# S4 convolution beside a SiLU feed-forward: the order of late loads on SyncE, a third weight landing buffer, and another split of the response's buffers

## The chip, the cores and the metric

The kernel runs on one core of one Trainium2 chip. The time is device microseconds (us) of one execution, taken as the median of three runs. Before the change it is 1117.28 us, and the three runs lie between 1115.24 and 1118.36 us. The profile was taken on one more execution, which took 1118.75 us.

The core has a matrix engine (TensorE, PE in the profile; PEld is its weight load), an elementwise engine (VectorE, DVE), an engine for activations and copies (ScalarE, ACT), GpSimd (POOL, used here to issue DMAs) and SyncE (SP, which only issues DMAs). Each engine takes its instructions in the order in which they were put into its queue. An instruction that waits holds up everything behind it on the same engine.

## The reference, cut to what matters

```python
xn = layernorm(x)                       # x: 2048 rows of 576
# A: S4 convolution over the 2048 positions, one filter per channel
K  = einsum("dn,dnl,dn->dl", C, exp(dt*A*l), dt*B).real      # 576 filters of length 2048
ya = irfft(rfft(pad(xn)) * rfft(pad(K)))[:2048] + xn * Dskip
# B: feed-forward, 576 -> 4608 -> 576
yb = silu(xn @ w1) @ w2
return x + ya + yb
```

## The kernel before, in words

**Feed-forward, the main thread.** The 2048 rows are worked in two halves of 1024, each half in two blocks of 512. The hidden width 4608 is cut into 9 chunks of 512, each of four pieces (`t` = 0 to 3) of 128. The loop goes over 36 blocks (half, chunk, block). `up` (lines 331 to 352) multiplies by `w1` into PSUM (`ph`) and applies SiLU (`gf`). `down` (lines 354 to 376) multiplies by `w2` into PSUM (`po`) and adds into the rows' accumulator (`acc`). All products are made of high and low parts, so a weight tile is split once it has landed: ScalarE casts the high part (`w1h`, line 303; `w2h`, line 324), VectorE subtracts for the low part (`w1l`, line 305; `w2l`, line 326). While one block is in `down`, `up` of the next block is already being made.

**Weights.** `load_w1` (line 274) brings two pieces of `w1` at a time into `w1r` with three DMAs on SyncE; it has one landing buffer. `load_w2` (line 310) brings one piece of `w2`, 288 KB, into `w2r` with one DMA on SyncE; it has two landing buffers, so a load waits until the split of the piece two places ahead has read its buffer. For the last chunk of the second half, the pieces 2 and 3 of `w2` and the second part of `w1` land in another pool (`yp`) instead. That pool takes the memory of the convolution's middle stage (`kl`), so those loads cannot start before that stage is over. All six weight loads of the last chunk are put into the program together, while the chunk before it is still at work (lines 435 to 438).

**Convolution, the side thread.** It is woven into the feed-forward at fixed fractions of its steps (`weave`, line 33, and `marks` and `tail_at` in `side`). Its stages are: layernorm and transposes; the filters (`kgen`), written to DRAM as `d1k`; the spectral stage (`spectral`, line 742); and the tail (`tail`, line 894). The spectral stage makes 16 visits `p`. In each, `load_k` fetches rows of `d1k` on GpSimd's queue, `halves` combines them on VectorE into `k` with one operation on line 782 and two on line 784, `response` multiplies `k` on TensorE (`pk`, line 795), `inputs` does the same for the data, and `back` writes a result to DRAM (`d2`, line 851). In the tail, `conv_load` (line 926) fetches rows of `d2` into a tile `ys` by two DMAs on SyncE, `load_r0` (line 898) fetches finished rows of the first half, and `add_conv` (line 935) makes the last small products (`py`, line 944) and adds them (line 952).

**What sets the order.** A scheduler orders the instructions of each engine when the program is built. An instruction can be tied to come after another one on the same engine: `behind(ins)`. The first eight `conv_load` calls and two `load_r0` calls of the tail stand in such a block:

```python
        with behind(pins["load"]):
            for j in (0, None, 2, None, None, None, None, None):
                conv_load()
                if j is not None:
                    load_r0(j)
```

`pins["load"]` is the weight load that was written last into the program at that time. Before the change every `load_w1` and `load_w2` sets it, and the last to do so ahead of the tail is piece 3 of the last chunk's `w2`. The tie only says that these loads come after that one load; it says nothing about the pieces of `w2` that were written earlier into the program and still wait for a landing buffer.

Of the kernel before, what the change touches and what calls it, by code (L numbers as in the profile page):

```python
# [11 lines left out]
F32 = mybir.dt.float32  # L12
# [3 lines left out]
ALU = mybir.AluOpType  # L16
# [3 lines left out]
P = 128  # L20
L = 2048
D = 576
# [21 lines left out]
def kernel(  # L44
# [22 lines left out]
    nc = tc.nc  # L67
    FT = 4
# [13 lines left out]
    d1k = dram.tile([32 * P, D], F32, name="d1k")  # L82
# [23 lines left out]
    wp = ctx.enter_context(tc.tile_pool(name="wp", bufs=2))  # L106
# [43 lines left out]
    pins = {}  # L150

    def behind(ins):
        return tc.issue_after(ins) if ins is not None else nullcontext()
# [113 lines left out]
    def ffn():  # L267
        w2v = w2.rearrange("(t p) d -> p t d", p=P)
# [5 lines left out]
        def load_w1(half, c, t):  # L274

            f = c * FT + t
            first = half == 0 and c == 0
            last = half == 1 and c == NCH - 1
            r1 = (pa if first and t else yp if last and t else wp).tile([P, 5, 2 * P], F32, tag="w1r", name="w1r", bufs=1)
            fs = slice(f * P, (f + 2) * P)  # L280
            v1 = w1[0:512, fs].rearrange("(k p) f -> p k f", p=P)
            eng = nc.sync
            if first and t == 0:
                eng = nc.scalar
                nc.sync.dma_start(r1[:, 0:2, :], v1[:, 0:2])
                eng.dma_start(r1[:, 2:4, :], v1[:, 2:4])
            else:
                nc.sync.dma_start(r1[:, 0:4, :], v1)  # L288
            if first and t == 0:
                eng = nc.gpsimd  # L290
            (eng if first and t == 0 else nc.sync).dma_start(r1[0:64, 4, :], w1[512:576, fs])  # L291
            pins["load"] = eng.dma_start(r1[64:128, 4, :], w1[512:576, fs]).ins  # L292
            R1[half, c, t] = r1

        def split_w1(half, c, t):
# [14 lines left out]
        def load_w2(half, c, t):  # L310

            first = half == 0 and c == 0
            last = half == 1 and c == NCH - 1
            r2 = (pa if first and t > 1 else yp if last and t > 1 else wp).tile([P, D], F32, tag="w2r", name="w2r", bufs=2)
            pins["load"] = nc.sync.dma_start(r2, w2v[:, c * FT + t, :]).ins  # L315
            R2[half, c, t] = r2

        def split_w2(half, c, t):
# [68 lines left out]
        def split_xt(b, kt):  # L387
            xh, xl, x4 = xts[2 + b]
            with behind(pins["gh"]):
# [3 lines left out]
                else:  # L393
                    r4 = R4.pop(b)
                    nc.scalar.copy(x4, r4)
                    nc.vector.tensor_sub(x4[64:, :], r4[64:, :], x4[64:, :])

        load_w1(0, 0, 0)
        yield 0
        load_w1(0, 0, 2)  # L400
        yield 0
        split_w1(0, 0, 0)
        yield 0
        split_w1(0, 0, 2)
        for t in range(FT):
            load_w2(0, 0, t)
# [12 lines left out]
        for i, blk in enumerate(blocks):  # L419
            half, c, b = blk  # L420
# [3 lines left out]
            if half == 0 and c == NCH - 1:  # L424
                next_xt(b)

            after = {
                (0, "u0"): [(load_w1, 0)],
                (0, "u1"): [(split_w1, 0), (load_w2, 0), (load_w2, 1)],
                (0, "u2"): [(load_w1, 2)],  # L430
                (1, "u0"): [(split_w1, 2), (split_w2, 0), (load_w2, 2)],
                (1, "d3"): [(split_w2, 1), (load_w2, 3), (split_w2, 2)],
                (1, "u2"): [(split_w2, 3)],
# [10 lines left out]
            for step in ("u0", "d0", "d1", "d2", "d3", "u1", "u2", "u3"):  # L444
                k = int(step[1])
# [12 lines left out]
    kl = yp = pa = tail_at = None  # L458
# [283 lines left out]
    def spectral():  # L742

        uv = d1u.rearrange("(m p r) d -> p r m d", m=2, r=P)
        kv = d1k.rearrange("(m p r) d -> p m r d", m=2, r=P)
        cwt = kl.tile([P, 16, 3], F32, name="cwt", bufs=1)
        nc.sync.dma_start(cwt, cw)
        us, ks, mats, kab, ys = {}, {}, {}, {}, {}
# [6 lines left out]
        def load_k(p):  # L755
            if p > 15:
                return
            t = kl.tile([P, 2, D], F32, tag="k", name="k")
            w = kl.tile([P, 2, D], F32, tag="kw", name="kw", bufs=1)
            nc.gpsimd.dma_start(t[:, 1], kv[p, 0])  # L760
            nc.gpsimd.dma_start(w[:, 0], kv[p, 1])
            for r in range(4):
                nc.gpsimd.dma_start(w[32 * r:32 * r + 32, 1], kv[p, 1, 32 * (r ^ 1):32 * (r ^ 1) + 32])
            ks[p] = t, w

        def load_m(p, i):
            if p > 15:
# [9 lines left out]
        def halves(p):  # L777
            if p > 15:
                return
            t, w = ks[p]  # L780
            c = cwt[:, p]
            nc.vector.scalar_tensor_tensor(w[:, 0], w[:, 1], c[:, 0:1], w[:, 0], op0=ALU.mult, op1=ALU.add)
            for m in range(2):
                nc.vector.scalar_tensor_tensor(t[:, m], w[:, 0], c[:, 1 + m:2 + m], t[:, 1], op0=ALU.mult, op1=ALU.add)

        def visit(p, t, name):

            banks = psb.tile([P, 2, 2, 512], F32, tag="psb", name=name)
            last = pins["pe"]
            for n, (h, g) in enumerate(((0, 1), (0, 0), (1, 1), (1, 0))):  # L790
                gs = slice(64 * g, 64 * g + 64)
                for o in range(4):
                    os = slice(32 * o, 32 * o + 32)
                    with tc.high_priority(), behind(last):
                        last = nc.tensor.matmul(banks[os, g, h, :HD], mats[p, 0][gs, os], t[gs, o % 2, h * HD:(h + 1) * HD],
                                                start=True, stop=True, tile_position=(64 * g, 32 * o),
                                                skip_group_check=True).ins
            pins["pe"] = last
            return banks

        def response(p):

            kas = [kl.tile([P, D], F32, tag="ka", name="ka") for _ in range(2)]
            clear(visit(p, ks.pop(p)[0], "pk"), kas)
            for g in range(2):
                ka, kb = kas[g], kl.tile([P, D], F32, tag="kb", name="kb")
                nc.scalar.mul(kb[:64], ka[64:], -1.0)
                nc.scalar.copy(kb[64:], ka[64:])
                nc.scalar.copy(ka[64:], ka[:64])
                kab[2 * p + g] = ka, kb  # L810

        def clear(banks, dsts):

            with tc.high_priority():
                for g in range(2):
                    nc.scalar.copy(dsts[g].rearrange("p (h d) -> p h d", h=2), banks[:, g, :, :HD])
# [36 lines left out]
        def load_u2(p):  # L853
            if p < 16:
                load_u(p)

        load_k(0)
        load_m(0, 0)
        load_u(0)
        yield 1.0  # L860
        with behind(pins["gh"]):
            halves(0)
        load_m(0, 1)
        load_m(1, 0)
        yield 1.03
        load_k(1)
        load_u(1)
        yield 1.05
        response(0)
        yield 1.07  # L870
        halves(1)
        yield 1.085
        inputs(0)
        load_k(2)
        yield 1.1
        for p in range(16):
            if p < 15:
                response(p + 1)
                load_m(p + 1, 1)
            load_k(p + 3)  # L880
            yield 1.1 + 0.9 * (3 * p + 1) / 48
            halves(p + 2)
            if p < 15:
                inputs(p + 1)
            load_u2(p + 2)
            yield 1.1 + 0.9 * (3 * p + 2) / 48
            back(p)
            load_m(p + 2, 0)
            yield 1.1 + 0.9 * (3 * p + 3) / 48
# [70 lines left out]
    def side():  # L960
# [69 lines left out]
        with tc.tile_pool(name="kl", bufs=2) as kl, tc.tile_pool(name="psb", bufs=1, space=PSUM) as psb:  # L1030
            for at in spectral():
                yield marks[1] + (at - 1) * (marks[2] - marks[1])
# [103 lines left out]
```

## Time and profile before

| What | Value |
|---|---|
| median of three runs | 1117.28 us |
| lowest, highest | 1115.24, 1118.36 us |
| the profiled execution | 1118.75 us |
| its span (first to last instruction) | 1116.9 us |
| mean granted clock of TensorE | 0.996 |

The span is what the profile's rows cover; the 1.85 us by which the profiled execution is longer lie around it. Rows of the timeline give a start in us from the span's beginning, a duration in us, the engine, the line of the kernel, the operation and "output<-input", how many instructions are merged in the row, and in brackets how long the engine had been idle before it and who released it. Rows of waits give the waiting engine and line, whom it waited for, the sum in us, the count and the longest. In rows of windows stand the stretch, its length, each engine's busy time and number of instructions, TensorE's granted clock, the share of the 16 DMA engines and GB/s. SPq is SyncE's queue of DMA issues.

### The profile page before, as it was taken

What the parts mean: (1) busy time and instruction counts of PE and PEld (TensorE: products, weight loads), DVE (VectorE), ACT (ScalarE), POOL (GpSimd) and SP (SyncE); (2) the same over time, 40 slices, a digit from 0 to 9 for tenths busy, and PEclk for the clock granted to TensorE, in tenths of its full rate; (3) what the DMA queues carried; (4) which work ended last, traced back from release to release, by engine and by line L of the source; (5) the groups of instructions that cost most, each with busy time, mean ns of one, the idle gap of its engine ahead of it and who ended that gap; (6) DMA issues with size and microseconds to landing.
All of it is one profiled execution on the core that took longest, in us unless ns stands there. A gap on an engine that the chain in (4) does not pass through costs nothing. (4 is left out here: it accounts for less than half of the span.)

```text
span 1116.9 us, 23956 instructions
## 1 busy us (share of the span) xinstructions
PE 1097.8 (98%) x9807; PEld 962.2 (86%) x9807; DVE 892.1 (80%) x1431; ACT 660.7 (59%) x1030; POOL 141.8 (13%) x257
## 2 busy tenths in 40 slices
PE   9999999999999999999999999999999999996998
PEld 7989998899989888989999987878888888896886
DVE  7799899999999999999999637867786867442443
ACT  4665466676777676667777437576767576431220
POOL 1100000000000000011000033332332321000111
PEclk9999999999999999999999999999999999998999
DMA  9746512525252434275734185554555644294363
GB/s 254 203 122 166 148 45 60 129 72 130 72 130 72 109 99 93 73 185 178 187 108 97 42 215 164 172 158 143 178 178 159 191 136 121 82 239 127 92 164 86
DMA packets 174397, 150.22 MB, mean 135 GB/s; under 512 B 112544, under 2 KB 144048, under 8 KB 174160
## 3 DMA queue, kind: packets, MB, share of 16 engines
q1 hardware_dynamic: 156544, 93.77, 32.9%
q0 software_dynamic: 16992, 54.07, 15.4%
q8 instruction: 77, 1.26, 0.5%
q10 hardware_dynamic: 752, 0.85, 0.3%
q14 instruction: 32, 0.26, 0.1%
HBM read 104.13 MB, written 44.61 MB: 133 GB/s over the span
## 5 line engine op out<-in xcount | busy, mean ns | idle before, releaser
L367 PE MATMUL po<-w2h,gh 128*128 128x288 f32 x1152 | 338.6, 298 | 10.2 <-ACT w2h L324 10.1
L367 PE MATMUL po<-w2l,gh 128*128 128x288 f32 x1152 | 339.4, 296 | 0.4 <-DVE w2l L326 0.4
L367 PE MATMUL po<-w2h,gl 128*128 128x288 f32 x1152 | 337.0, 295 | 0.8 <-DVE gl L352 0.8
L367 PEld LDWEIGHTS po<-w2h,gh 128*128 128x128 f32 x1152 | 215.4, 188 | 26.9 <-ACT w2h L324 11.5
L367 PEld LDWEIGHTS po<-w2l,gh 128*128 128x128 f32 x1152 | 216.5, 188 | 7.8 <-issue 1.4
L367 PEld LDWEIGHTS po<-w2h,gl 128*128 128x128 f32 x1152 | 215.8, 188 | 3.3 <-issue 1.4
L349 ACT ACTIVATE gf<-ph 128x512 f32<-128x512 f32 (+1 forms) x146 | 85.7, 588 | 155.7 <-PE ph L343 145.8
L371 DVE TENSOR_TENSOR acc<-po,acc 128x288 f32<-128x288 f32 x288 | 125.9, 451 | 51.0 <-PE po L367 49.7
L341 PE MATMUL ph<-xh,w1h 128*128 128x512 f32 (+1 forms) x584 | 162.1, 390 | 0.0
L341 PE MATMUL ph<-xh,w1l 128*128 128x512 f32 (+1 forms) x584 | 159.7, 387 | 0.0
L341 PE MATMUL ph<-xl,w1h 128*128 128x512 f32 (+1 forms) x584 | 158.7, 387 | 0.0
L352 DVE TENSOR_TENSOR gl<-gf,gh 128x512 fp32r<-128x512 f32 (+1 forms) x148 | 98.6, 671 | 74.1 <-ACT gh L350 73.2
L341 PEld LDWEIGHTS ph<-xl,w1h 128*128 128x128 f32 x584 | 107.1, 188 | 21.5 <-issue 0.9
L341 PEld LDWEIGHTS ph<-xh,w1l 128*128 128x128 f32 x584 | 106.9, 188 | 21.0 <-issue 0.9
L341 PEld LDWEIGHTS ph<-xh,w1h 128*128 128x128 f32 x584 | 104.2, 188 | 18.1 <-issue 1.4
L350 ACT CAST gh<-gf 128x512 fp32r<-128x512 f32 (+1 forms) x148 | 89.3, 608 | 23.5 <-PE po L367 20.7
L174 POOL DMA_DIRECT2D d1u<-u x32 | 17.4, 545 | 463.5 <-ACT u L173 463.5
L326 DVE TENSOR_TENSOR w2l<-w2r,w2h 128x576 fp32r<-128x576 f32 x72 | 53.2, 750 | 18.7 <-ACT w2h L324 18.5
L324 ACT CAST w2h<-w2r 128x576 fp32r<-128x576 f32 x72 | 47.0, 672 | 31.6 <-DMA w2r<-in_B_w_dram 24.4
L663 ACT ACTIVATE c<-th,magic 128x1040 f32<-128x1040 f32 x36 | 42.1, 1168 | 37.1 <-DVE C L686 27.5
L832 ACT CAST yh<-y 128x576 fp32r<-128x576 f32 x32 | 21.6, 674 | 65.1 <-DVE y L829 53.2
L665 ACT ACTIVATE c<-th 128x1040 f32<-128x1040 f32 x36 | 38.7, 1075 | 32.8 <-DVE th L664 32.8
(196 smaller groups left out, 1779.4 us busy)
## 6 DMA issues: line engine op xcount, KB each, us to landing
w2r<-in_B_w_dram SPq DMA_DIRECT2D x72, 288.0 KB, 4.1
w1r<-in_B_w_dram SPq DMA_DIRECT2D x35, 512.0 KB, 4.0
d1u<-u POOLq DMA_DIRECT2D x32, 288.0 KB, 2.7
d1k<-stage SPq DMA_DIRECT2D x36, 256.0 KB, 4.7
u<-d1u POOLq DMA_DIRECT2D x16, 576.0 KB, 4.7
d<-yo POOLq DMA_DIRECT2D x32, 288.0 KB, 3.0
ys<-d SPq DMA_DIRECT2D x32, 288.0 KB, 7.1
xr<-dxn SPq DMA_DIRECT2D x16, 288.0 KB, 2.9
```

The costliest lines, as they stand in the source:

```text
L174: nc.gpsimd.dma_start(d1u.rearrange("(p m j) d -> m j p d", m=2, j=NJ)[m, j], u1)
L324: pins["w2h"] = nc.scalar.copy(h2, r2).ins
L326: pins["w2l"] = nc.vector.tensor_sub(l2, r2, h2).ins
L341: nc.tensor.matmul(ph, w[:, kt, :], v[:, kt, a:e], start=n + kt == 0, stop=False)
L349: nc.scalar.activation(gf, ph, AF.Silu)
L350: pins["gh"] = nc.scalar.copy(gh, gf).ins
L352: pins["gl"] = nc.vector.tensor_sub(gl, gf, gh).ins
L367: pins["pe"] = nc.tensor.matmul(po[:, :HD], G[blk, t][g][:, js], W2[half, c, t][w][:, hs], start=n == 0, stop=n == 3 * FT - 1).ins
L371: nc.vector.tensor_add(acc[j][:, hs], po[:, :HD], acc[j][:, hs])
L663: nc.scalar.activation(c65, th, AF.Identity, bias=magic)
L665: nc.scalar.activation(c65, th, AF.Abs)
L832: nc.scalar.copy(yh, y)
```

## The change

Three things are changed.

1. `pins["load"]` is no longer set by `load_w1`, and by `load_w2` only for the pieces 0 and 1. When the tail is written, it therefore is piece 1 of the last chunk's `w2`, which lands in a regular `w2r` buffer.
2. The regular `w2r` buffers become three. Where the pieces 2 and 3 land in another pool, in the first and the last chunk, there are two as before.
3. In the spectral stage, the tile `kw` holds all three row sets that `halves` needs and has two buffers; the output tile `k` has one buffer and is taken when `halves` runs. Before, `k` had two buffers and one of the row sets was loaded straight into it, and `kw` had one. The two plain loads of 288 KB become one of 576 KB; the four loads of 72 KB stay.

```diff
-            pins["load"] = eng.dma_start(r1[64:128, 4, :], w1[512:576, fs]).ins
+            eng.dma_start(r1[64:128, 4, :], w1[512:576, fs])
...
-            r2 = (pa if first and t > 1 else yp if last and t > 1 else wp).tile([P, D], F32, tag="w2r", name="w2r", bufs=2)
-            pins["load"] = nc.sync.dma_start(r2, w2v[:, c * FT + t, :]).ins
+            r2 = (pa if first and t > 1 else yp if last and t > 1 else wp).tile([P, D], F32, tag="w2r", name="w2r", bufs=2 if t > 1 and (first or last) else 3)
+            landed = nc.sync.dma_start(r2, w2v[:, c * FT + t, :]).ins
+            if t < 2:
+                pins["load"] = landed
...
-        kv = d1k.rearrange("(m p r) d -> p m r d", m=2, r=P)
+        kv = d1k.rearrange("(m p r) d -> p r m d", m=2, r=P)
...
-            t = kl.tile([P, 2, D], F32, tag="k", name="k")
-            w = kl.tile([P, 2, D], F32, tag="kw", name="kw", bufs=1)
-            nc.gpsimd.dma_start(t[:, 1], kv[p, 0])
-            nc.gpsimd.dma_start(w[:, 0], kv[p, 1])
+            w = kl.tile([P, 3, D], F32, tag="kw", name="kw")
+            nc.gpsimd.dma_start(w[:, 0:2], kv[p])
             for r in range(4):
-                nc.gpsimd.dma_start(w[32 * r:32 * r + 32, 1], kv[p, 1, 32 * (r ^ 1):32 * (r ^ 1) + 32])
-            ks[p] = t, w
+                nc.gpsimd.dma_start(w[32 * r:32 * r + 32, 2], kv[p, 32 * (r ^ 1):32 * (r ^ 1) + 32, 1])
+            ks[p] = w
...
-            t, w = ks[p]
+            w, t = ks[p], kl.tile([P, 2, D], F32, tag="k", name="k", bufs=1)
+            ks[p] = t
             c = cwt[:, p]
-            nc.vector.scalar_tensor_tensor(w[:, 0], w[:, 1], c[:, 0:1], w[:, 0], op0=ALU.mult, op1=ALU.add)
+            nc.vector.scalar_tensor_tensor(w[:, 2], w[:, 2], c[:, 0:1], w[:, 1], op0=ALU.mult, op1=ALU.add)
             for m in range(2):
-                nc.vector.scalar_tensor_tensor(t[:, m], w[:, 0], c[:, 1 + m:2 + m], t[:, 1], op0=ALU.mult, op1=ALU.add)
+                nc.vector.scalar_tensor_tensor(t[:, m], w[:, 2], c[:, 1 + m:2 + m], w[:, 0], op0=ALU.mult, op1=ALU.add)
...
-            clear(visit(p, ks.pop(p)[0], "pk"), kas)
+            clear(visit(p, ks.pop(p), "pk"), kas)
```

## The prediction

> **What bounds the kernel now.** I read the page's busy times first, then who waits for whom on TensorE, then the timeline of the one long wait, on TensorE, ScalarE and SyncE.
>
> ```profile
> PE 1097.8 (98%) x9807; PEld 962.2 (86%) x9807; DVE 892.1 (80%) x1431; ACT 660.7 (59%) x1030; POOL 141.8 (13%) x257
> ```
> ```profile
> PE po L367 <- ACT w2h L324: 10.1, 4, 8.6
> ...
> PE po L367 <- DVE gl L352: 0.8, 1, 0.8
> ...
> PE po L367 <- DVE w2l L326: 0.4, 1, 0.4
> ```
>
> TensorE is the bound: only what shortens its own queue or its waits counts. The change takes no matmul away, so its prize can only lie in the waits, and one of them, 8.6 us, is most of what there is. It is here:
>
> ```profile
> 1010.47 0.61 PE L341 MATMUL ph<-xh,w1h 128*128 128x512 f32 x2
> 1019.73 1.09 PE L367 MATMUL po<-w2h,gh 128*128 128x288 f32 x3 [8.65 <-ACT w2h L324]
> ```
> ```profile
> 994.48 0.68 ACT L324 CAST w2h<-w2r 128x576 fp32r<-128x576 f32 x1 [6.88 <-PE po L367]
> 997.89 0.67 ACT L324 CAST w2h<-w2r 128x576 fp32r<-128x576 f32 x1 [2.73 <-DMA w2r<-in_B_w_dram]
> ...
> 1005.59 0.62 ACT L350 CAST gh<-gf 128x512 fp32r<-128x512 f32 x1
> 1019.01 0.67 ACT L324 CAST w2h<-w2r 128x576 fp32r<-128x576 f32 x1 [12.79 <-DMA w2r<-in_B_w_dram]
> ```
> ```profile
> 977.82 1.06 SPq L315 DMA_DIRECT2D w2r<-in_B_w_dram  x2
> 978.92 2.55 SPq L932 DMA_DIRECT2D ys<-d  x2
> 981.52 0.61 SPq L900 DMA_DIRECT2D r<-dr  x1
> 982.17 1.90 SPq L932 DMA_DIRECT2D ys<-d  x3
> 984.17 0.54 SPq L288 DMA_DIRECT2D w1r<-in_B_w_dram  x1
> 985.53 0.35 SPq L315 DMA_DIRECT2D w2r<-in_B_w_dram  x1
> ...
> 992.72 13.40 SPq L932 DMA_DIRECT2D ys<-d  x10
> 1006.63 1.58 SPq L900 DMA_DIRECT2D r<-dr  x2
> 1009.10 11.73 SPq L315 DMA_DIRECT2D w2r<-in_B_w_dram  x3
> ```
>
> Read backwards: TensorE stands until the cast at 1019.01, ScalarE stood 12.79 us for the data of that cast, and its DMA was issued at 1009.10, behind sixteen `ys` loads and four `r0` loads. The w2 pieces are consumed in the program's order, four to a chunk; the last chunk's four come after these, so the casts at 994.48, 997.89 and 1019.01 are the pieces 1, 2 and 3 of the last chunk but one. Pieces 2 (985.53) and 3 (1009.10) had no landing buffer yet when the last chunk's pieces 2 and 3 (977.82) found theirs in `yp`, and `behind` ties the convolution rows to that last piece alone. So the rows went ahead.
>
> **The change, part by part.**
>
> *The stall.* With the tie on piece 1 of the last chunk, SyncE must issue, before any convolution row, that load and all that share its buffers ahead of it: piece 3 of the chunk before, then pieces 0 and 1. With three buffers, piece 2 no longer waits for anything in this stretch, and piece 3 needs only the buffer of piece 0, which is split about 981 to 983 (below). It is issued by about 984, some 24 us earlier than now. Even at 12.3 us, the longest landing of a w2r load from 880 on, it is there by 997; its cast can take the place behind the `gh` cast that ends at 1006.2, ahead of the 1011.1 at which TensorE now stops. The term is the whole wait, **8.65 us**.
>
> ```profile
> 981.27 0.67 ACT L324 CAST w2h<-w2r 128x576 fp32r<-128x576 f32 x1
> ```
> ```profile
> DMA to landing us min/median/max: 2.7/4.5/12.3
> ```
>
> *The clock after the stall.* The stall also costs half-speed matmuls behind it:
>
> ```profile
> 979.00:1009.00 30.00, 30.00 (x182) 27.39 (x181) 11.42 (x20) 9.04 (x15) 0.00 (x0) 1.00 1.07 237
> 1011.08:1019.73 8.65, 0.00 (x2) 0.00 (x1) 0.02 (x1) 0.72 (x2) 0.00 (x0) 0.77 0.65 208
> 1019.73:1022.76 3.03, 3.03 (x12) 2.84 (x13) 1.98 (x4) 2.32 (x4) 0.00 (x0) 0.53 0.33 97
> ```
>
> The granted clock is 1.00 before, and 0.53 in the 3.03 us after. The loss is 3.03 x (1 - 0.53) = **1.42 us**, which goes with the stall. The Trainium skill, page "TensorE: Matmul & The Clock Gate", Part 1, says the clock falls to half after an idle window of about 3.4 us and comes back after about as much sustained work; by its figure the term would be an estimated 3.4 / 2 = 1.7 us and the sum below 0.3 us larger. The trace agrees in kind (0.53) and has the shorter recovery (3.03 us).
>
> *The third buffer elsewhere.* The other three waits of TensorE for `w2h` sum to 10.1 - 8.6 = 1.5 us, and the one for `w2l` is 0.4. In each chunk, piece 3 is loaded only after the split of piece 1, just ahead of its own use; with a third buffer it comes a split earlier. The wait for `gl`, 0.8 us, is one for VectorE, whose queue the spectral part touches. Ends: all 2.7 us go, or, since a new order of instructions makes small waits of its own, none do. I take half, **1.3 us**, because most of it hangs on loads that come earlier for certain while the number of new waits is unknown.
>
> *The convolution rows.* The added tie makes sixteen `ys` and four `r0` loads wait behind piece 1 of the last chunk, whose buffer comes free with the split of piece 2. That split ended at 998.60 + 0.76 in the old order:
>
> ```profile
> 998.60 0.76 DVE L326 TENSOR_TENSOR w2l<-w2r,w2h 128x576 fp32r<-128x576 f32 x1 [2.28 <-ACT w2h L324]
> ```
> ```profile
> r<-dr SPq DMA_DIRECT2D x4, 576.0 KB, 10.2
> ```
> ```profile
> 1039.47 1.23 PE L944 MATMUL py<-ys,s 64*32 64x288 f32 x32
> ```
>
> So the rows start at 997 to 1000 instead of 978.92. The first `add_conv` (1039.47, some 10 us earlier after the change: 1029) needs two `ys` tiles, and its VectorE adds need one `r0` tile: the first five DMAs, issued within 2.55 + 0.61 + 1.90 us in the old order, landing in about 10. They are there by 1016, with 13 us to spare. The stretch's DMA engines are full (share 1.07, 237 GB/s); the bytes are the same, only later. Cost: nothing. If that cover were gone, it would be TensorE waiting for `py`, priced under the rivals. Nothing else is queued on SyncE behind the rows until the store rows of the tail.
>
> *The spectral buffers.* VectorE's three operations per visit stay, of the same shape. GpSimd issues one DMA less per visit, on an engine busy 13%: nothing. The merged load has the size of the `u` load and so lands later than a plain one by the difference of these rows, 4.7 - 3.3 = 1.4 us, but its second buffer lets it be issued a visit earlier.
>
> ```profile
> u<-d1u POOLq DMA_DIRECT2D x16, 576.0 KB, 4.7
> ...
> kw<-d1k POOLq DMA_DIRECT2D x16, 288.0 KB, 3.3
> ```
> ```profile
> DVE k L784 <- DMA k<-d1k: 16.8, 11, 3.1
> ```
> ```profile
> POOL k L760 <- PE pk L795: 38.1, 12, 5.4
> ```
> ```profile
> 873.75 1.20 PE L795 MATMUL pk<-k,m 64*32 64x288 f32 x32
> ...
> 892.10 1.20 PE L795 MATMUL pk<-k,m 64*32 64x288 f32 x32
> ```
> ```profile
> 880.32 0.81 DVE L784 SCALAR_TENSOR_TENSOR k<-kw,cwt,k 128x576 f32<-128x576 f32 x1
> ```
>
> The old order is: TensorE frees a `k` buffer (`pk` ends about 875), GpSimd, which waited for that, loads into it, VectorE waits for the landing (16.8 us over 11 visits) and ends line 784 at 881.1. With one `k` buffer, VectorE waits for `pk` itself, without the load in between, and what it writes is read by the next `pk`, at 892.10, instead of the one after. That leaves 892.1 - 881.1 = 11 us. The bounds of the new wait: a gain of the 16.8 us on VectorE (no gain on TensorE beyond the 0.8 already counted), or a loss if VectorE takes over GpSimd's 38.1 us (rival below). I take nothing, because the nearest row has the new wait ending before the old one did.
>
> *Sum.* 8.65 + 1.42 + 1.3 = 11.4 us off the profiled execution's 1118.75 gives 1107.4. That execution is 1.5 us over the median of 1117.28, so for the median I predict 1117.28 - 11.4 = **1106 us**.
>
> **The rivals.**
>
> *The VectorE queue is caught on the single `k` buffer (slower).* VectorE takes line 784 in its fixed order; if TensorE's `pk` runs later than the scheduler thought, `gl` and `acc` work stands behind it and TensorE waits for them. GpSimd's waits for `pk` are 38.1 / 12 = 3.2 us each. If VectorE bears them in 15 visits, that is 48 us, and if TensorE feels half, 24 us: 1117.3 - 11.4 + 24 = 1130. It decides from 11.4 / 15 = 0.76 us per visit. For it: VectorE is busy 80%, and TensorE has waited for its `gl` once already, 0.8 us. Against it: the 11 us above, and VectorE's own waits of 1.5 us each (16.8 / 11), which were behind the same `pk` plus a load, cost TensorE almost nothing.
>
> *The rows come too late.* If the first `add_conv` needed the whole first batch (978.92 to 1008.2 for the issues, then 10.2 for the last landing, 39 us in all), it would be ready at 997 + 39 = 1036 and TensorE would stand 1036 - 1029 = 7 us: 1106 + 7 = 1113. Against: it needs the first five of them.
>
> *The change doesn't do what it says.* Piece 3 could still be issued behind the rows, or be early while another operand of the same stretch comes late in its stead: 1117. Against: the tie reaches piece 3 through the shared buffers, and the one long wait of TensorE names `w2h` alone.
>
> **How the numbers follow.** The forecast's case has 0.78, late rows 0.05, no effect 0.06, the caught VectorE queue or another order that costs more than it gives 0.11. About 0.3%, 3.4 us, is what a measurement of this kernel can tell: faster means under 1113.9, slower over 1120.6. Faster takes the first two cases: 0.83; same 0.06; slower 0.11. The likeliest case's own range is from all small waits gone (8.65 + 1.42 + 2.7 = 12.8: 1104.5, less 1.5 for the spread of the runs) to none gone (10.1: 1107.2) with new small waits of 2 us: 1103 to 1109. I widen it to 1103 to 1112 to take in part of the late rows.
>
> **What would show it.** Right: TensorE's longest wait for `w2h` under 1 us; no 0.5 clock after the start and before the end; on SyncE four w2r loads ahead of the first `ys`, which is issued after 995; first `py` near 1029 without a wait; VectorE's wait for `k` loads gone. Wrong: `ys` rows between the w2r loads again; TensorE waiting for `py`, or for `gl` and `acc` between 660 and 950 while VectorE waits for `pk` at line 784.

## The result, and the profile after

The changed kernel takes 1106.61 us (median of six runs, 1105.45 to 1106.98), the kernel before, run beside it, 1117.74 us. The ratio is 0.9901, with a 95% interval of 0.9884 to 0.9918: faster by 11.1 us. The span of the profiled executions fell from 1116.9 to 1104.8 us.

The page's busy times and TensorE's waits after the change. Each run's rows carry the line numbers of its own kernel; behind line 315 they differ by one or two from those of the kernel before.

```profile
PE 1095.5 (99%) x9807; PEld 961.4 (87%) x9807; DVE 891.6 (81%) x1431; ACT 659.5 (60%) x1030; POOL 136.2 (12%) x241
```
```profile
PE po L369 <- DVE acc L373: 2.1, 3, 0.7
PE pz L979 <- DVE zero L974: 1.3, 1, 1.3
PE pt L134 <- DVE xn L212: 1.0, 2, 0.9
PE py L945 <- DVE r L953: 0.5, 1, 0.5
PE po L369 <- DVE gl L354: 0.2, 1, 0.2
```

The wait for `w2h` is gone altogether, in its long form and in its three short ones. A new wait, for `acc`, stands in the list with 2.1 us. TensorE's waits sum to 5.1 us, where they were 14.2: 9.1 of the 12.1 us of the span. TensorE's busy time is 2.3 us shorter, of which the half clock behind the old stall explains 1.42. The other 0.9 us of busy time and the last 0.7 us of the span I did not follow.

SyncE's timeline in the stretch that held the stall, then ScalarE's casts of the same pieces, then two windows behind it (engines in the order PE, PEld, DVE, ACT, POOL, then the granted clock, the DMA share and GB/s):

```profile
984.68 1.06 SPq L315 DMA_DIRECT2D w2r<-in_B_w_dram  x2
...
987.70 0.58 SPq L315 DMA_DIRECT2D w2r<-in_B_w_dram  x1
...
996.73 1.97 SPq L315 DMA_DIRECT2D w2r<-in_B_w_dram  x2
998.75 1.27 SPq L933 DMA_DIRECT2D ys<-d  x2
```
```profile
984.91 0.67 ACT L326 CAST w2h<-w2r 128x576 fp32r<-128x576 f32 x1
995.25 0.66 ACT L326 CAST w2h<-w2r 128x576 fp32r<-128x576 f32 x1
996.33 1.25 ACT L326 CAST w2h<-w2r 128x576 fp32r<-128x576 f32 x2
```
```profile
1000.00:1010.00 10.00, 10.00 (x66) 9.37 (x65) 2.76 (x6) 1.98 (x4) 0.00 (x0) 1.00 1.00 245
...
1020.00:1030.00 10.00, 10.00 (x63) 8.18 (x69) 3.50 (x5) 3.88 (x7) 0.00 (x0) 1.00 0.95 239
```
Then the first `py` of TensorE:

```profile
1029.61 1.22 PE L945 MATMUL py<-ys,s 64*32 64x288 f32 x32
```

Piece 3 of the last chunk but one is issued at 987.70 instead of 1009.10, pieces 0 and 1 of the last chunk follow at 996.73, and only then the rows, at 998.75. The pieces 2 and 3 are cast back to back at 996.33, with no wait for a DMA. About the same DMA load as before (share 0.95 to 1.00, 239 to 245 GB/s, against 1.07 and 237) now runs under a TensorE that is full at clock 1.00, and the first `py` finds its rows without a wait at 1029.61.

### The profile page after: what moved, and what is told of

The parts are those of the page before. It is cut to its first block, busy times and chain, and to the rows that moved or that the text cites. A ratio compares the mean times of both kernels' runs of the same rounds, so it can differ in the third digit from the quotient of the medians.

```text
span 1104.8 us, 23941 instructions
## 1 busy us (share of the span) xinstructions
PE 1095.5 (99%) x9807; PEld 961.4 (87%) x9807; DVE 891.6 (81%) x1431; ACT 659.5 (60%) x1030; POOL 136.2 (12%) x241
## 4 chain that ended last, share of the span: by engine, by line
PE 80%; DVE 10%; DMA 4%; ACT 2%; POOL 1%; issue 1%; DVEq 0%; ACTq 0%; POOLq 0%
PE po L369 35%; PE ph L343 30%; PE kp L708 3%; DMA kw<-d1k 3%; PE ph L344 3%; PE ph L345 2%; PE z L723 2%; DVE y L829 1%; PE pb L847 1%; DVE y L830 1%; PE pu L171 1%; DVE k L785 1%; DVE acc L373 1%; POOL kw L763 1%; DVE y L827 1%
## 5 line engine op out<-in xcount | busy, mean ns | idle before, releaser
L343 PE MATMUL ph<-xh,w1h 128*128 128x512 f32 (+1 forms) x584 | 159.5, 389 | 0.0
L305 DVE TENSOR_TENSOR w1l<-w1r,w1h 128x640 fp32r<-128x640 f32 x72 | 57.0, 819 | 0.2
L344 PE MATMUL ph<-x,w1h 128*128 128x512 f32 (+1 forms) x146 | 56.6, 388 | 0.0
```

The lines of the kernel that those rows point to most:

```text
L305: pins["w1l"] = nc.vector.tensor_sub(l1, src, h1).ins
L343: nc.tensor.matmul(ph, w[:, kt, :], v[:, kt, a:e], start=n + kt == 0, stop=False)
L344: nc.tensor.matmul(ph, h1[:, 4, :], x4[:, a:e], start=False, stop=False)
```

## The experiments

The change has three parts: the tie, the third `w2r` buffer and the spectral buffers. Six runs complete the eight combinations, two repeat one of them and the full change, and two more take other causes apart. Ratios are against the kernel before on the same chip, with 95% intervals; the microseconds are the ratio's distance from 1 times 1117.7.

| tie | third buffer | spectral | ratio | us against before |
|---|---|---|---|---|
| x | | | 0.9912 [0.9891, 0.9934] | -9.8 |
| | x | | 0.9918 [0.9895, 0.9940] | -9.2 |
| | | x | 1.0034 [1.0019, 1.0049] | +3.8 |
| x | x | | 0.9920 [0.9895, 0.9945]; again 0.9929 [0.9914, 0.9944] | -8.9; -7.9 |
| x | | x | 0.9962 [0.9949, 0.9976] | -4.2 |
| | x | x | 0.9904 [0.9887, 0.9921] | -10.7 |
| x | x | x | 0.9901 [0.9884, 0.9918]; again 0.9902 [0.9887, 0.9917] | -11.1; -11.0 |

**The tie alone.**

```diff
-            pins["load"] = eng.dma_start(r1[64:128, 4, :], w1[512:576, fs]).ins
+            eng.dma_start(r1[64:128, 4, :], w1[512:576, fs])
...
-            pins["load"] = nc.sync.dma_start(r2, w2v[:, c * FT + t, :]).ins
+            landed = nc.sync.dma_start(r2, w2v[:, c * FT + t, :]).ins
+            if t < 2:
+                pins["load"] = landed
```

> Only the tie is changed: the convolution rows come after piece 1 of the last chunk's w2; w2r keeps two buffers, the spectral stage is as before. Theory 'the order on SyncE makes the stall': piece 3 of the chunk before is issued after the split of piece 1, near 996 us instead of 1009, with nothing of the rows ahead of it, lands within 5 us, and TensorE's 8.65 us wait and the half clock after it go: 1117.3 - 10.1 = 1107 us, the small waits for w2h between 640 and 980 us (about 1.5 us) stay. Rival 'the third buffer is needed': with two buffers piece 3 still comes late for its cast, a wait of 3 to 5 us is left: 1111 to 1113 us.

The time is 1108.55 us, ratio 0.9912. SyncE's timeline and TensorE's waits between 640 and 980 us:

```profile
995.64 4.66 SPq L315 DMA_DIRECT2D w2r<-in_B_w_dram  x3
1000.35 1.28 SPq L934 DMA_DIRECT2D ys<-d  x2
```
```profile
PE po L369 <- ACT w2h L326: 2.0, 2, 1.1
PE po L369 <- DVE w2l L328: 0.4, 1, 0.4
```

Piece 3 is issued at 995.64, as its theory had it (the first of the three loads in that row), and the long wait and the half clock are gone. The small waits for `w2h` stay. The third buffer is not needed for the stall.

**The third buffer alone.**

```diff
-            ... tag="w2r", name="w2r", bufs=2)
+            ... tag="w2r", name="w2r", bufs=2 if t > 1 and (first or last) else 3)
```

> Only the third w2r buffer; the rows stay tied to the last chunk's piece 3 and the spectral stage is as before. Theory 'any way of issuing piece 3 early will do': with a third buffer its load waits only for the split of piece 0 and stands where piece 2 stood before, near 985 us, with a few rows ahead of it; even at 12 us of landing it is there by 998: stall and half clock gone, and the small w2h waits with them: 1105 to 1107 us. Rival 'only the tie keeps the rows from delaying it' (full DMA engines, share 1.07): it lands late all the same and most of the stall stays: 1113 to 1117 us.

The time is 1109.28 us, ratio 0.9918. SyncE, ScalarE, and TensorE between 640 and 980 us:

```profile
986.12 1.28 SPq L932 DMA_DIRECT2D ys<-d  x2
...
989.41 1.09 SPq L315 DMA_DIRECT2D w2r<-in_B_w_dram  x1
992.18 4.79 SPq L932 DMA_DIRECT2D ys<-d  x3
```
```profile
1000.34 0.68 ACT L324 CAST w2h<-w2r 128x576 fp32r<-128x576 f32 x1 [3.02 <-DMA w2r<-in_B_w_dram]
```
```profile
PE po L367 <- DVE acc L371: 1.6, 2, 1.0
PE po L367 <- ACT gh L350: 1.0, 1, 1.0
```

Piece 3 is issued in the middle of the rows and cast some 11 us later, and that is soon enough. So the tie is not needed either: each of the two alone removes the stall, and their gains do not add. The time is 2 us above the range that the theory gave. The small waits show the second finding: with a third buffer those for `w2h` go, and others of the same size (2.6 us) come.

**The spectral buffers alone.** The diff is the part of the change from `kv` to `response`.

> Only the spectral stage's buffers (kw two, k one, one merged load). Theory of the prediction: hidden work, no effect by itself, the 8.65 us stall stays: 1116 to 1118 us. Rival 'it makes the spectral stage end later' (in the changed kernel the first load into the yp pool is issued at 983.05 us instead of 976.19): the rows, and the w2 piece behind them, come up to 7 us later, so the stall grows to up to 15 us: 1119 to 1124 us. Rival 'VectorE is caught on the single k buffer': new waits of TensorE between 660 and 950 us, slower by their sum.

The time is 1122.47 us, ratio 1.0034: slower. It lies in the range of the first rival, but not for its reason: the rows do start later (988.90), and yet the stall is shorter, not longer. TensorE's longest waits in sum, of the whole run, and ScalarE around 884 us:

```profile
PE po L367 <- ACT w2h L324: 8.3, 3, 6.6
PE po L367 <- ACT gh L350: 2.5, 1, 2.5
PE po L367 <- DVE acc L371: 1.8, 3, 1.0
```
```profile
884.09 0.67 ACT L324 CAST w2h<-w2r 128x576 fp32r<-128x576 f32 x1 [2.63 <-DMA w2r<-in_B_w_dram]
884.67 0.59 ACT L349 ACTIVATE gf<-ph 128x512 f32<-128x512 f32 x1
885.28 0.68 ACT L806 ACTIVATE kb<-ka 64x576 f32<-64x576 f32 x1
...
888.05 0.62 ACT L350 CAST gh<-gf 128x512 fp32r<-128x512 f32 x1
```

The stall is there, somewhat shorter (6.6 us). The loss is in the spectral stage, and its largest wait is for `gh`: ScalarE stands 2.63 us for a late piece 3 of `w2`, the SiLU behind it is late, four copies of `kb` have their place ahead of its `gh` cast, and TensorE waits 2.5 us for `gh`. VectorE waits only 1.8 us for `pk` in the spectral stage, so the single `k` buffer is hardly what costs. TensorE's waits for `acc` (1.8 us) and `ut` (1.2 us) are new too.

**Tie and spectral buffers, and third buffer and spectral buffers.**

> The full change without the third w2r buffer: tie and spectral buffers. In the run with the spectral buffers alone, ScalarE stood 2.6 us at 884 us for the late piece 3 of a chunk's w2 and TensorE then waited 2.5 us for gh. Theory 'that cost is the two-buffer w2r load caught in the new order': it stays here, TensorE's small waits between 640 and 980 us sum to 6 us or more, and the time is 1110 to 1112 us (1107 to 1108.5 of the tie alone plus 3 to 4). Rival 'the spectral buffers cost nothing by themselves': 1107 to 1108 us.

> The full change without the tie: third w2r buffer and spectral buffers. Theory 'a third buffer makes the tie superfluous': piece 3 is issued soon after the split of piece 0 and no long wait is there: 1106 to 1108 us, as the full change. Rival 'the tie is what holds it': a wait of several us near 1011 us: 1112 us or more. If the cost of the spectral buffers comes from late w2 loads, their small waits (2.5 us for gh at 886 us) are gone here too.

With the tie the time is 1113.81 us (0.9962), with the third buffer 1107.32 us (0.9904). TensorE's waits between 640 and 980 us, ScalarE ahead of the longest of them and the clock after it, with the tie; then TensorE's longest wait in the same stretch with the third buffer:

```profile
PE po L369 <- ACT gh L352: 2.3, 1, 2.3
PE po L369 <- DVE gl L354: 0.9, 1, 0.9
PE po L369 <- ACT w2h L326: 0.8, 1, 0.8
PE pb L847 <- ACT ut L817: 0.8, 1, 0.8
PE po L369 <- DVE acc L373: 0.7, 1, 0.7
```
```profile
880.89 0.67 ACT L326 CAST w2h<-w2r 128x576 fp32r<-128x576 f32 x1 [2.68 <-DMA w2r<-in_B_w_dram]
```
```profile
885.00:889.00 4.00, 3.48 (x13) 3.36 (x14) 1.54 (x3) 3.90 (x7) 0.12 (x1) 0.57 0.94 290
```
```profile
PE po L367 <- DVE acc L371: 2.4, 3, 0.9
```

With two `w2r` buffers the `gh` wait comes back, 2.3 us, again behind a `w2` piece for which ScalarE stands (2.68 us), and after it the clock falls to 0.57 over 4 us, which costs another 4 x 0.43 = 1.7 us. With three buffers neither is there. So 4.0 of the 5.6 us by which the spectral buffers slow the kernel with the tie go with a `w2` piece that lands late for the order that they bring about, and the third buffer takes them away. The rest was not followed: the profiled execution, 1111.86 us, is the fastest of its six. ScalarE's order also differs from build to build, so that the late piece alone makes the wait is argued. The tie turns out superfluous beside the third buffer: 0.9904 without, 0.9901 with.

**Tie and third buffer, twice, and the full change again.**

> Tie and third buffer, spectral stage as before. Theory 'the spectral part gives and costs nothing': 1106 to 1107 us, the same as the full change (1106.6), with TensorE's small waits for acc (2.1 us) perhaps gone. Rival 'the spectral part gives something': 1108 us or more. Rival 'the spectral part costs something': 1104 us or less. The first load into the yp pool is at 976 if the later 983 of the changed kernel comes from the spectral part, and at 983 if it comes from the other two.

> The full change again, beside the same without its spectral part, on one chip: 1106.6 us as measured. Theory 'the spectral part is worth nothing or little where w2r has three buffers': within 2 us of the run without it. Rival 'it gains about 2 us': its interval lies below that of the run without it.

> Tie and third buffer without the spectral part, again beside the full change. 1108 to 1110 us as in the first run, with the 2.4 us wait for acc at 705 us and the half clock behind it (3.4 us) in its profile if both belong to the kernel's order and not to that one execution; without them it equals the full change.

Without the spectral part: 1109.94 us (0.9920), and beside the full change 1109.63 us (0.9929, 0.9914 to 0.9944). The full change: 1106.99 us (0.9902, 0.9887 to 0.9917). The intervals overlap by 0.0003, so the spectral part most likely gains some 2 to 3 us where `w2r` has three buffers. The first load into `yp` is at 985.2 us here, at 983.4 with the third buffer alone and at 985.3 with the spectral part alone, but at 975.9 with the tie alone: either buffer change makes an order in which the spectral stage ends later. What that costs by itself no run shows. One profiled execution without the spectral part took 1109.45 us and shows what can be lost there (VectorE, TensorE's wait, and the windows around it); the other, of 1107.64 us, has shorter waits for `acc` there (1.5 us in two) and no half clock behind them:

```profile
701.96 0.82 DVE L784 SCALAR_TENSOR_TENSOR kw<-kw,cwt 128x576 f32<-128x576 f32 x1 [2.84 <-DMA kw<-d1k]
```
```profile
PE po L369 <- DVE acc L373: 2.4, 1, 2.4
```
```profile
704.80:707.20 2.40, 0.00 (x0) 0.00 (x0) 2.34 (x5) 0.00 (x0) 2.40 (x5) 0.97 0.45 127
707.20:710.50 3.30, 3.27 (x13) 3.27 (x14) 3.08 (x5) 1.75 (x3) 1.35 (x4) 0.50 0.60 166
```

VectorE stands 2.84 us for `kw` rows, `acc` work is late behind it, TensorE waits 2.43 us, and 3.3 us at half clock follow: 4.1 us in all. With one `kw` buffer this wait on GpSimd's loads depends on the execution: in the other one VectorE stands 1.60 us for the same rows. That this is the whole of the 2 to 3 us is argued, not shown.

**Six row buffers in the kernel before.**

```diff
-            yss[j] = yp.tile([P, 4, HD], F32, tag="ys", name="ys", bufs=8)
+            yss[j] = yp.tile([P, 4, HD], F32, tag="ys", name="ys", bufs=6)
```

> The kernel before with six ys buffers instead of eight: four ys loads less (4 x 0.295 MB) stand ahead of piece 3 on SyncE, nothing else of the order changes there. Theory 'the stall is the time of the loads ahead': at 237 GB/s they take 5.0 us, so piece 3 is issued near 1004 instead of 1009.1 and TensorE's wait falls from 8.65 to about 3.7 us; the time falls by 5 us plus whatever the clock gives back: 1110 to 1112 us. Rival 'piece 3 waits for its buffer or for the full DMA engines, not for the queue': wait and time stay, 1116 to 1118 us.

The time is 1117.69 us, ratio 0.9985 (0.9967 to 1.0004): no change clear of noise. Two of its ten runs took 1111.35 and 1112.32 us (mean clock 0.998 and 1.000), the other eight 1116.6 to 1120.0 (0.994 to 0.997); no profile shows what the two lack. SyncE, ScalarE and TensorE:

```profile
1003.28 11.51 SPq L315 DMA_DIRECT2D w2r<-in_B_w_dram  x3
```
```profile
1012.98 0.67 ACT L324 CAST w2h<-w2r 128x576 fp32r<-128x576 f32 x1 [11.10 <-DMA w2r<-in_B_w_dram]
```
```profile
1006.15 0.29 PE L367 MATMUL po<-w2l,gh 128*128 128x288 f32 x1
1013.70 0.85 PE L367 MATMUL po<-w2h,gh 128*128 128x288 f32 x2 [7.26 <-ACT w2h L324]
```

The first half of the theory holds: with four loads less ahead, piece 3 is issued 5.8 us earlier (5.0 expected) and cast 6.0 us earlier. The second half falls: TensorE's wait shrinks by 1.4 us alone, because TensorE arrives at it 4.6 us earlier (1006.44 instead of 1011.08). In the kernel before, it still made `ph` products ahead of the wait, up to 1011.08; here these have their place behind it. The wait is the end of the piece's cast less TensorE's arrival, and the order that decides the arrival is made anew with every build. That the scheduler put less ahead because it took the piece to be there earlier is argued.

**The rows on GpSimd's queue in the kernel before.**

```diff
-    def conv_load():
+    def conv_load(eng=nc.sync):
...
-                nc.sync.dma_start(yss[j][64 * h:64 * h + 64],
+                eng.dma_start(yss[j][64 * h:64 * h + 64],
...
-                conv_load()
+                conv_load(nc.gpsimd)
```

The last two lines are those in `tail`, for the first eight row tiles.

> The kernel before with the sixteen first ys loads issued by GpSimd instead of SyncE; same loads, same time, w2r keeps two buffers and no tie is added. Theory 'the order in SyncE's queue makes the stall': piece 3 is issued right after the split of piece 1, near 996 us, and the stall goes though the DMA engines are as full as before: 1107 to 1109 us. Rival 'the full DMA engines make it': piece 3 lands 10 us or more after its issue, past 1007, and part of the stall stays: 1110 us or more.

The time is 1123.61 us, ratio 1.0052 (1.0037 to 1.0068): slower. GpSimd, SyncE, ScalarE and TensorE:

```profile
976.12 5.54 POOL L932 DMA_DIRECT2D ys<-d  x9 [3.12 <-DMA d<-yo]
```
```profile
983.96 11.58 SPq L291 DMA_DIRECT2D w1r<-in_B_w_dram  x1
995.64 2.90 SPq L315 DMA_DIRECT2D w2r<-in_B_w_dram  x1
```
```profile
1013.44 0.67 ACT L324 CAST w2h<-w2r 128x576 fp32r<-128x576 f32 x1 [19.01 <-DMA w2r<-in_B_w_dram]
```
```profile
PE ph L341 <- ACT gf L349: 13.6, 1, 13.6
```

The theory that the order in SyncE's queue alone makes the stall falls, and the rival holds in kind. With the rows off that queue, nine of them are issued within 5.5 us from 976 on, and the weights suffer. A single issue of a `w1` load holds SyncE for 11.58 us (0.50 in the kernel before), so piece 2 is issued at 995.64 instead of 985.53, and then it takes 17.7 us to land (12.3 before). It is cast at 1013.44. ScalarE stands in front of it with SiLU work behind, and TensorE waits 13.6 us.

Why the rows did less harm on SyncE's own queue can be read in the chain of the kernel before (start, duration, what):

```profile
998.45 10.58 DMA ys<-d
1009.03 0.02 issue
1009.05 0.02 SPq L315
```

SyncE comes to piece 3 the moment a row load has landed that it issued eight places earlier, at 998.45. In the same way the row load at 997.83 follows the landing of piece 2 at 997.82, which was issued eight places before it. So in this trace SyncE sends rows and weights only as fast as earlier loads land, about 10 us each, which is why sixteen rows hold piece 3 back for so long. On GpSimd's queue the rows wait, after the first nine, for each other's landings alone (2.77 us for the tenth), and SyncE's loads come beside them. That this is what makes the weights land later is argued. What the runs show is that the tie or an earlier free buffer brings piece 3 in time, and that another queue for the rows does the opposite.

## Why the prediction was right

**The stall, 8.65 us, and the clock, 1.42 us.** Both went, by the mechanism given: piece 3 at 987.70 (by about 984 was forecast), and no half clock between the start and the end. The tie alone measured 9.8 us (7.4 to 12.2 by its interval), against 10.1 for these two terms. Piece 3 came later than forecast because it does wait for the buffer of piece 0, as reasoned, but piece 0 was cast at 984.91 here, not at 981.27.

**The convolution rows at no cost.** Right: rows at 998.75 (997 to 1000 forecast), first `py` at 1029.61 (1029) without a wait. The rival of late rows has nothing in the trace.

**The third buffer elsewhere, 1.3 us.** This step was mis-sized. All waits for `w2h` and `w2l` went, as reckoned, but new ones came: the small waits of this kind sum to 2.3 us after (`acc` 2.1, `gl` 0.2), against 2.7 before, a gain of 0.4 us. The lower end, "none", was closer. And the prediction did not say that the third buffer alone would have removed the stall.

**The spectral buffers at nothing.** It costs nothing in the whole change, as forecast, but the forecast is wrong for the part on its own. Alone the part costs 3.8 us, with the tie 5.6 (0.9962 against 0.9912), and with three `w2r` buffers it costs nothing and most likely gains 2 to 3 us. The rival named the wrong engine: as far as the traces show, it was not VectorE on the single `k` buffer but ScalarE on a late `w2` piece. Of the sign given for that rival, one half is there (TensorE waits 2.1 us for `acc`) and the other is not (VectorE has no wait for `pk` in that stretch). The forecast that VectorE's wait for `k` loads goes held, since nothing is loaded into `k` any more; its wait for `kw` grew from 5.4 to 11.6 us, less than the 16.8 us that went:

```profile
DVE kw L783 <- DMA kw<-d1k: 11.6, 5, 5.4
```

So the total of 11.4 us came close to the measured 11.1 partly by luck, because two errors cancelled. The tie and the third buffer without the spectral part, for which the terms add up to 11.4, measured 8.9 and 7.9 us: 2.5 to 3.5 too little, of which the third buffer's small waits explain 0.9. The spectral part, taken as nothing, most likely gave 2 to 3.

**The clock.** The Trainium skill, page "TensorE: Matmul & The Clock Gate", Part 1, has the clock fall to half after an idle window of about 3.4 us. The trace agrees for the stall: half clock stood behind the wait of 8.65 us and went with it. But two runs had the clock at half after waits shorter than that window, 2.43 and 2.3 us.

## What to carry to other kernels

When a load of operands is late, look at what was allowed ahead of it: a tie to "the last load in the program" does not cover loads that were written earlier and still wait for a buffer. Moving the bulk to another queue made it worse here, with the DMA engines full (share 1.04 to 1.07); holding it back, or freeing the operand's buffer earlier, removed the wait. One wait can be removed by either of two changes whose gains do not add, and a part that is harmless in the whole may be harmful alone, so combinations have to be measured.

## What was not expected of the hardware

A wait of TensorE of only 2.4 us was followed by about 3.3 us at half clock in one execution (clock 0.50 from 707.20 to 710.50 in the windows above), and one of 2.3 us in another kernel (0.57 over 4 us). A wait of 2.5 us, which ended at 888.7 in the run with the spectral buffers alone, was not (the window behind it):

```profile
888.00:892.00 4.00, 3.28 (x19) 2.97 (x20) 1.33 (x3) 3.88 (x8) 0.36 (x1) 1.00 1.04 320
```

So a short wait may cost nothing more, or as much again as a whole small optimisation gains.
